# Attention and top-1 experts on one core: the leftover rows of an expert move into that expert's own pass, small units share one tile, and the fallback leaves GpSimd out

## The chip, the core and the metric

The kernel runs on one core of a Trainium2 chip. The metric is device time in microseconds; the kernel before has a median of 573.84 us over three runs. The profile is one further execution of the same kernel, with a span of 555.2 us between its first and last instruction, and all times inside the kernel are counted from the start of that span. The engines are TensorE (PE in the profile, its weight loads PEld), VectorE (DVE), ScalarE (ACT), GpSimd (POOL) and SyncE (SP). A `q` behind an engine's name stands for its sequencer, which handles waits, branches and register work.

## The reference

A banded attention is followed by a layer of eight experts, of which each token uses one. Cut to what matters:

```python
def reference(...):
    # attention: q, k, v of (4 batches, 8 heads, 768 positions, 64)
    scores = q @ k.T / 8 + bias           # per head a slope times the distance
    a = softmax(where(is_global | is_local, scores, -1e9))   # 8 global keys, 96 local ones
    x = (a @ v) -> (3072, 512)            # heads side by side
    # experts
    logits = x @ w_gate                   # (3072, 8)
    expert = argmax(logits)               # one expert per token
    gate = softmax(logits)[expert]
    for e in range(8):
        rows = x[expert == e]
        out[expert == e] = gate * (relu(rows @ w1[e]) @ w2[e])   # 512 -> 1024 -> 512
```

Everything is fp32.

## The kernel before

The kernel first does the attention and the routing (0 to about 168 us in the profile), writing each token's row to a table in DRAM, sorted by expert. A row of that table has 516 words: 512 of x, the gate, the token's number and two of padding. Two single tiles of 128 rows, of experts 0 and 1, are taken early. Then come eight passes, one per expert. A pass handles 256 rows (two tiles) with a recursive matrix product that trades multiplications for additions; that is `up_a`, `up_b` (first layer) and `down_a`, `down_b` (second layer). What an expert has beyond that is done by plain products, in units of 128, 64 and 32 rows. Which of the units are needed is a number from 0 to 7, the form: bit 4 for the unit of 128 rows, bit 2 for that of 64, bit 1 for that of 32. It depends on the data, so the kernel has a body of code for each form and chooses with a jump table, the switch.

```python
    def gather_u(self, e):                       # rows of the units, from DRAM
        for i in range(3):                       # 128, 64 and 32 rows: a tile each
            self.gather(self.xs[:, i, :], self.grow[:, e, 2 + i:3 + i])

    def x_units(self):                           # transposes on TensorE
        banks = self.t
        for c in range(NDC):                     # NDC = 4
            nc.tensor.transpose(banks[0][:, c, :], self.xs[:, 0, ts(c, P)], ident[:])      # L1136
        for s, cols in self.COLS.items():        # s = 1: 64 rows, s = 2: 32 rows
            n = P >> s
            for c in range(NDC):
                nc.tensor.transpose(banks[1][:, c, cols], self.xs[0:n, s, ts(c, P)],       # L1140
                                    ident[0:n, 0:n])
        nc.scalar.copy(self.xsT[0][:], banks[0][:])
        nc.scalar.copy(self.xsT[1][:, :, r], banks[1][:, :, r])                            # L1143

    def units(self, e, k, banks, between):       # the body for form k
        small = [s for s in (1, 2) if k >> 2 - s & 1]
        big = range(2 if k & 4 else 0)
        for s in small:
            ...  matmul into ph                                                            # L1157
            nc.scalar.activation(self.hr[s - 1][:], ph, AF.Relu)
        for half in big:
            ...  up_s (L853), relu
        between[0]()                             # a part of the pass's own work
        for s in small:
            ...  transpose hr (L1168), copy on ScalarE
        between[1]()                             # another part of it
        for half in big:
            self.down_s(e, self.huT, half, banks[2])                                       # L863
        ...
        for s in small:
            ...  matmul into py (L1182), scaled by the gate on ScalarE (L1185)

    def hint(self, e):                           # asks for a prefetch of the body to come
        if e < E:
            tc.switch_hint({PE: self.forms[e]}, FORMS, label=f"units{e}")

    def by_form(self, e, banks, between):
        for k in tc.Switch({eng: self.forms[e] for eng in self.ENGINES}, FORMS, hint=f"units{e}"):
            self.units(e, k, banks, between)     # ENGINES = (PE, ACT)
        self.hint(e + 1)
        self.send_u(e)                           # three scatters on GpSimd

    def passes(self, judge):
        for e in range(E):
            ...  up_a(e, 0), up_a(e, 1)
            if e == 0:
                self.x_units(); self.meta_u(0); self.gather_u(1)
            ...  up_b(e, 0), up_a(e, 2), up_b(e, 1)
            parts = lambda: (self.up_a(e, 3), self.up_copy(3)), lambda: self.up_b(e, 2)
            if e == 0:
                self.by_form(0, self.u[0:2] + self.d, parts)     # expert 0's units
            ...
            if more:
                self.x_units(); self.meta_u(e + 1)               # the NEXT expert's units
                if e + 2 < E: self.gather_u(e + 2)
            ...  up_b(e, 3), h_combine(1)
            parts = (first half of down_a, second half of down_a)            # L1076
            if more:
                self.by_form(e + 1, self.u, parts)               # the NEXT expert's units
            ...
            if more: self.x_in(e + 1); self.x_combine()          # L994
            self.gated(e); self.down_b(e)                                    # L1085
            ...  results, weights of e + 2 fetched
            for t in range(2): self.send(e, t)                   # scatters on GpSimd, L793
```

So pass 0 has two switches, passes 1 to 6 one each, for the next expert, and pass 7 none. After the passes, a flag is read on every engine, and where the fast path is not valid for the data, a general version runs:

```python
    flag = nc.values_load(bad_i[0:1, 0:1], min_val=0, max_val=1, ...)          # L1345, all engines
    with tc.If(flag > 0, preferred_fallthrough_block=False):                   # L1347
        again = Route("_g")
        ...  general(stack, again)       # attention anew, uses GpSimd
        ...  experts(stack, again, wpool)
```

With the reference's inputs the flag is zero and the general version is not run.

Of the kernel before, what the change touches and what calls it, by code (L numbers as in the profile page):

```python
# [23 lines left out]
def kernel(  # L24
# [28 lines left out]
    NA = E  # L53
    NB = NTOK // P - 1
    JT = NA + NB
# [82 lines left out]
    def weights(wpool, expert):  # L138
        w1t = wpool.tile([P, NDC, F], F32, tag="w1", name="w1t")
        w2t = wpool.tile([P, NFC, DM], F32, tag="w2", name="w2t")  # L140

        def fill():
            for dst, src, n in ((w1t, moe_w1, NDC), (w2t, moe_w2, NFC)):
                s = src[ds(expert, 1)].rearrange("o (c p) f -> p (o c) f", p=P)
                for a in range(0, n, n // 2):
                    nc.sync.dma_start(out=dst[:, a:a + n // 2, :], in_=s[:, a:a + n // 2, :])

        return w1t, w2t, fill


# [21 lines left out]
    def choose(pool, rt, xr, lg):  # L172
# [13 lines left out]
        def gates():  # L186
            nc.scalar.activation(sh[:], sh[:], AF.Exp)
            se = pool.tile([P, NBLK], F32, tag="se", name="se")
            nc.vector.tensor_reduce(se[:], sh[:], AX.X, ALU.add)
            nc.vector.tensor_scalar(se[:], se[:], 1e-9, None, ALU.add)  # L190
            nc.vector.reciprocal(xr[:, :, DM:DM + 1], se[:].unsqueeze(2))
            nc.vector.tensor_copy(out=xr[:, :, DM + 1:DM + 2].bitcast(I32), in_=rt.tokid[:].unsqueeze(2))
            nc.vector.tensor_scalar(rt.tokid[:], rt.tokid[:], S, None, ALU.add)

        return oh, gates
# [293 lines left out]
    def block_logits(pool, ps, wg, xr, lg, i):  # L489
        pt = ps.tile([P, NDC, P], F32, tag="t", name="pt")  # L490
        for c in range(NDC):
            nc.tensor.transpose(pt[:, c, :], xr[:, i, ts(c, P)], ident[:])
        xt = pool.tile([P, NDC, P], F32, tag="xt", bufs=2, name="xt")
        nc.scalar.copy(xt[:], pt[:])
        pl = ps.tile([P, 512], F32, tag="t", name="pl")
        for c in range(NDC):
            nc.tensor.matmul(pl[:, 0:E], lhsT=xt[:, c, :], rhs=wg[:, c, :],
                             start=(c == 0), stop=(c == NDC - 1))
        nc.vector.tensor_copy(out=lg[:, i, :], in_=pl[:, 0:E])


    def general(stack, rt):
        wg = stack.enter_context(tc.tile_pool(name="wg", bufs=1)).tile([P, NDC, E], F32, name="wg")
        nc.scalar.dma_start(out=wg[:], in_=moe_w_gate.rearrange("(c p) e -> p c e", p=P))
        pool, rows = router_pools(stack)
        seq = stack.enter_context(tc.tile_pool(name="seq_g", bufs=1))
        work = stack.enter_context(tc.tile_pool(name="work_g", bufs=2))
        ps_s = stack.enter_context(tc.tile_pool(name="ps_sg", bufs=2, space=bass.MemoryType.PSUM))
# [4 lines left out]
        key = seq.tile([P, S], F32, name="key_g")  # L513
        nc.gpsimd.iota(key[:], pattern=[[1, S]], base=0, channel_multiplier=0,
                       allow_small_or_imprecise_dtypes=True)

        with tc.For_i(0, B, 1) as b:
            kt = seq.tile([P, NPAIR, S], F32, name="kt_g")
            qt = seq.tile([P, NPAIR, S], F32, name="qt_g")
            vt = seq.tile([P, NBLK, H, D], F32, name="vt_g")  # L520
            for i in range(NBLK):
                for nm, src, dst, on, scale in (("k", k, kt, "dve", 1.0), ("q", q, qt, "act", QS)):
                    r = work.tile([P, H, D], F32, tag=nm, name=f"raw_{nm}g")
                    nc.sync.dma_start(out=r[:], in_=src[ds(b, 1), :, ts(i, P), :].rearrange(
                        "o h p d -> p (o h) d"))
                    transposed(ps_t, dst[:, :, ts(i, P)], r, on, scale)
                nc.sync.dma_start(out=vt[:, i], in_=v[ds(b, 1), :, ts(i, P), :].rearrange(
                    "o h p d -> p (o h) d"))
            xr, lg = new_rows(rows)
            units = [(i, h) for i in range(NBLK) for h in range(H)]  # L530
            st = {}

            def scores(u):
                i, h = units[u]
                if h == 0:
                    rel = work.tile([P, S], F32, tag="rel", name="rel_g")
                    nc.gpsimd.iota(rel[:], pattern=[[-1, S]], base=i * P, channel_multiplier=1,
                                   allow_small_or_imprecise_dtypes=True)
                    st["mask"] = mask(work, rel[:], key[:], S)
                    st["sums", i] = work.tile([P, H], F32, tag="sums", name="sums_g")  # L540
                keep, dist, neg = st["mask"]
                m, r = h // 2, slice(D * (h % 2), D * (h % 2) + D)
                sp = ps_s.tile([P, 2, 512], F32, tag="s", name="sp_g")
                for a in range(2):
# [46 lines left out]
    def experts(stack, rt, wpool):  # L591
# [120 lines left out]
        with tc.manual_schedule(engines={PE}):  # L712
# [5 lines left out]
            for j in range(JT):  # L718
# [3 lines left out]
                if j:  # L722
                    down(j - 1)
# [660 lines left out]
```

## Time and profile before

| | |
|---|---|
| median of 3 runs | 573.84 us (571.16 to 578.95) |
| span of the profiled execution | 555.2 us |
| attention and routing, 0 to about 190 us | TensorE busy 179.42 of 190.00 us |
| 190.0 to 254.5 us, early tiles and pass 0 | TensorE busy 56.59 of 64.50 us |
| 254.5 to 511.0 us, passes 1 to 6 | TensorE busy 251.19 of 256.50 us |
| 511.0 to 555.0 us, pass 7 and the end | TensorE busy 24.73 of 44.00 us |
| transposes of the small units (L1140) | 64 matmul records, 6.6 us |
| GpSimd's gathers of the units' rows (L785, `xs`) | 24, mean 1148 ns of GpSimd each |

How to read it: an engine's share of busy time is an average over stages. TensorE is nearly always busy in passes 1 to 6, less in pass 0 and not at all in the last 19 us. The profile counts neither branches nor waits nor register work as busy; they are found in the trace under the line they belong to. Those of the switch's dispatch and exit, and those of the closing of the program, all carry the kernel's last line, L1379.

### The profile page before, as it was taken

The numbers are of one execution on the slowest core, as the hardware profiler recorded it, in microseconds if no ns is written. First come the engines' busy times: TensorE is split into PE (matmuls) and PEld (weight loads), VectorE is DVE, ScalarE is ACT, GpSimd is POOL, SyncE is SP. The second block draws the span as 40 slices with busy tenths as digits, with TensorE's granted clock in tenths as the row PEclk, the third lists the DMA queues.
The fourth block names the chain that finished last, engine by engine and source line by source line (L and its number), as shares of the span: only waits on it lengthen the run. The fifth ranks groups of instructions, "written<-read, shape, count | busy, mean of one in ns | idle before, by whom it ended". The sixth has DMA issues, their size and how long they took to land.

```text
span 555.2 us, 12977 instructions
## 1 busy us (share of the span) xinstructions
PE 511.9 (92%) x5377; PEld 435.9 (79%) x5377; DVE 301.5 (54%) x638; ACT 146.2 (26%) x281; POOL 160.0 (29%) x242
## 2 busy tenths in 40 slices
PE   5899999999999999679999999999899999997950
PEld 4788898888987786469969969978787996987940
DVE  5566866767865451626708706817804641764810
ACT  3544555444441012111202211211211211221210
POOL 5200231311514560633206206306303411603010
PEclk9999999999999999899999999999999999998995
DMA  9998999999961320524524506506503621600010
GB/s 179 216 197 198 252 255 208 223 269 242 236 203 77 101 79 21 183 84 153 182 77 169 170 1 238 201 4 227 198 2 115 215 87 32 220 3 32 13 44 2
DMA packets 99314, 77.84 MB, mean 140 GB/s; under 512 B 80054, under 2 KB 80056, under 8 KB 99200
## 3 DMA queue, kind: packets, MB, share of 16 engines
q1 hardware_dynamic: 90368, 56.63, 40.0%
q0 software_dynamic: 8000, 19.77, 10.6%
q8 instruction: 59, 0.97, 0.8%
q14 instruction: 55, 0.45, 0.3%
q10 hardware_dynamic: 832, 0.02, 0.1%
HBM read 63.54 MB, written 14.73 MB: 141 GB/s over the span
## 4 chain that ended last, share of the span: by engine, by line
PE 86%; DVE 4%; issue 3%; ACT 2%; DMA 1%; POOL 0%; ACTq 0%; POOLq 0%; DVEq 0%
PE u L1014 18%; PE d L1076 10%; PE u L853 9%; PE sp L358 7%; PE d L1085 7%; PE po L387 6%; PE u L863 6%; PE pt L239 4%; PE pr L398 3%; PE u L1157 3%; PE u L1182 3%; PE d L863 3%; PE px L417 2%; PE t L994 1%; DVE p L372 1%
## 5 line engine op out<-in xcount | busy, mean ns | idle before, releaser
L372 DVE TENSOR_TENSOR p<-sp,other 128x1024 f32<-128x1024 f32 x40 | 47.1, 1219 | 33.7 <-PE sp L358 31.8
L1092 DVE TENSOR_TENSOR UV<-UV,d 128x512 f32<-128x512 f32 x8 | 5.5, 687 | 103.5 <-ACT yu L1185 70.4
L793 POOL DMA_INDIRECT out_dram<-ys,to_u x8 | 8.3, 1038 | 154.5 <-ACT yu L1185 115.8
L853 PEld LDWEIGHTS u<-xsT,w 128*128 128x128 f32 x448 | 50.7, 192 | 1.7 <-DVE ch L1062 0.8
L853 PE MATMUL u<-xsT,w 128*128 128x128 f32 x448 | 51.7, 276 | 0.0
L1014 PE MATMUL u<-cx,c 128*128 128x128 f32 x384 | 48.1, 275 | 0.0
L1014 PEld LDWEIGHTS u<-cx,c 128*128 128x128 f32 x384 | 45.5, 192 | 0.0
L379 ACT ACTIVATE p<-p 128x1024 f32<-128x1024 f32 (+1 forms) x48 | 44.5, 977 | 2.1 <-DVE p L372 2.0
L358 PE MATMUL sp<-qt,kt 64*128 64x128 f32 x448 | 39.0, 281 | 1.4 <-DVE kt L244 1.4
L1014 PE MATMUL u<-xT,w 128*128 128x128 f32 x256 | 40.1, 279 | 0.1
L785 POOL DMA_INDIRECT xs<-xs_dram,grow x24 | 27.5, 1148 | 34.8 <-PE t L1140 28.9
L387 PE MATMUL po<-p,vt 128*64 128x128 f32 x448 | 37.1, 274 | 0.0
L1014 PEld LDWEIGHTS u<-xT,w 128*128 128x128 f32 x256 | 34.2, 192 | 1.9 <-issue 0.7
L300 POOL COPY ka<-kt 128x384 f32<-128x384 f32 x16 | 8.2, 511 | 93.7 <-DVE den_all L423 90.7
L863 PE MATMUL u<-w,huT 128*128 128x512 f32 x80 | 35.1, 592 | 0.0
L358 PEld LDWEIGHTS sp<-qt,kt 64*128 64x128 f32 x448 | 31.9, 193 | 3.4 <-ACT qt L242 1.6
L1076 PE MATMUL d<-c,ch 128*128 128x256 f32 x128 | 32.8, 379 | 0.0
L1045 DVE TENSOR_TENSOR uv<-uv,u 128x256 f32<-128x256 f32 x32 | 13.4, 420 | 31.4 <-ACT uv L1041 18.3
L219 POOL DMA_INDIRECT xs_dram<-xr,slot_i x24 | 23.7, 986 | 22.6 <-DVE base_e L217 9.8
L1041 ACT COPY uv<-u 128x256 f32<-128x256 f32 x32 | 11.9, 372 | 68.4 <-PE u L1014 68.3
L863 PEld LDWEIGHTS u<-w,huT 128*128 128x128 f32 x80 | 15.2, 190 | 17.0 <-issue 16.7
L793 POOL DMA_INDIRECT out_dram<-y,to x16 | 18.1, 1134 | 35.3 <-DVE y L1103 31.3
(233 smaller groups left out, 1057.4 us busy)
## 6 DMA issues: line engine op xcount, KB each, us to landing
w<-in_moe_w_dram SPq DMA_DIRECT2D x24, 1024.0 KB, 5.6
w<-in_moe_w_dram SPq DMA_DIRECT2D x16, 512.0 KB, 6.3
raw_q<-in_q_dram SPq DMA_DIRECT2D x24, 256.0 KB, 5.4
raw_k<-in_k_dram SPq DMA_DIRECT2D x24, 256.0 KB, 5.4
vt<-in_v_dram SPq DMA_DIRECT2D x24, 256.0 KB, 6.2
va<-vt SPq DMA_DIRECT2D x16, 192.0 KB, 5.6
va<-vt SPq DMA_DIRECT2D x16, 64.0 KB, 5.2
xs_dram<-xr,slot_i POOLq DMA_INDIRECT x24, 6.2
```

What stands on the lines that cost most here:

```text
L219: d = nc.gpsimd.indirect_dma_start(out=xs_dram[:], out_offset=bass.IndirectOffsetOnAxis(ap=slot_i[:, u:u + 1], axis=0), in_=xr[:, u, :].bi ...
L358: nc.tensor.matmul(sp[:, a, j, t, :], lhsT=kt[r, m, :], rhs=qts[n][r, m, :], start=True, stop=True, skip_group_check=True)
L372: nc.vector.tensor_tensor(z, sc, bi, ALU.add)
L379: nc.scalar.activation(z, z, AF.Exp)
L387: nc.tensor.matmul(po[D * a:D * a + D, m, :], lhsT=vt[:, 2 * m + a, :], rhs=ps[n][m // 2][:, a, m % 2, t, :], start=(x == 0), stop=(x == l ...
L785: nc.gpsimd.indirect_dma_start(out=dst.bitcast(I32), out_offset=None, in_=xs_dram[:], in_offset=bass.IndirectOffsetOnAxis(ap=idx, axis=0), ...
L793: d = nc.gpsimd.indirect_dma_start(out=out.rearrange("n (g d) -> (n g) d", g=parts), out_offset=bass.IndirectOffsetOnAxis(ap=idx, axis=0), ...
L853: nc.tensor.matmul(ph[:, i, :], lhsT=self.w[e % 2][0][:, c, ts(half * HF + i, P)], rhs=xT[:, c, :], start=(c == 0), stop=(c == NDC - 1), s ...
L863: nc.tensor.matmul(py[:].rearrange("p a b -> p (a b)"), lhsT=h[:, f, :], rhs=self.w[e % 2][1][:, f, :], start=(f == 0), stop=(f == NFC - 1 ...
L1014: nc.tensor.matmul(bank[:, r, :], lhsT=lhs(k), rhs=rhs(k), start=first, stop=True, skip_group_check=True)
L1076: nc.tensor.matmul(self.half(i, j), lhsT=lhs, rhs=rhs, start=(f == 0 and j == 0), stop=True, skip_group_check=True)
L1085: nc.tensor.matmul(self.half(i, j), lhsT=lhs(f), rhs=rhs(f), start=False, stop=True, skip_group_check=True)
```

## The change

The change has four parts.

* **Own expert's form.** Pass e now runs the units of expert e, not of e + 1, in its second-layer stage. Every pass has exactly one switch, in the same place, and pass 0's extra switch is gone.
* **Small units in one tile.** The rows of the 64-row and the 32-row unit are gathered into one tile of 96 rows, so that 4 transposes do for both. The gates and token numbers are wanted on partitions 0 to 63 and 0 to 31, so they are gathered a second time, into a small tile `mu`, 4 words a row.
* **Forms rotated.** Body number k of the switch now holds form (k + 6) mod 8, so the bodies lie in memory in the order 6, 7, 0, 1, 2, 3, 4, 5.
* **Fallback without GpSimd.** The general version is written anew, unrolled, without any GpSimd work, and the flag is read on the other four engines only.

The core of the diff:

```diff
         def gather(self, dst, idx):
+            n = dst.shape[-1]
             nc.gpsimd.indirect_dma_start(
-                out=dst.bitcast(I32), out_offset=None, in_=xs_dram[:],
+                out=dst.bitcast(I32), out_offset=None, in_=xs_dram[:].rearrange("r (a b) -> (r a) b", b=n),
...
+            nc.vector.tensor_copy(out=k_i[:], in_=k[:])
+            nc.vector.tensor_scalar(k[:], k[:], float(FORMS - FIRST), None, ADD)     # FIRST = 6
             nc.vector.tensor_copy(out=self.form[:], in_=k[:])
+            nc.vector.tensor_scalar(self.form[:], self.form[:], FORMS - 1, None, ALU.bitwise_and)
...          (seven small VectorE operations that make the indices grow_m and grow_e)
         def gather_u(self, e):
-            for i in range(3):
-                self.gather(self.xs[:, i, :], self.grow[:, e, 2 + i:3 + i])
+            self.gather(self.xs[:, 0, :], self.grow[:, e, 2:3])
+            self.gather(self.xs[:, 1, :], self.grow_m[:, e:e + 1])
+            for i in (1, 2):
+                self.gather(self.mu[:, i, :], self.grow_e[:, e, i - 1:i])

         def meta_u(self, e):
-            f = self.to_f
-            nc.gpsimd.tensor_copy(out=f[:], in_=self.xs[:, :, DM + 1].bitcast(I32))
+            f, mu = self.to_f, self.mu
+            nc.gpsimd.tensor_copy(out=mu[:, 0, :], in_=self.xs[:, 0, DM:XW])
+            nc.gpsimd.tensor_copy(out=f[:], in_=mu[:, :, 1].bitcast(I32))
...
-            for s, cols in self.COLS.items():
-                n = P >> s
-                for c in range(NDC):
-                    nc.tensor.transpose(banks[1][:, c, cols], self.xs[0:n, s, ts(c, P)], ident[0:n, 0:n])
+            n = self.COLS[2].stop
+            for c in range(NDC):
+                nc.tensor.transpose(banks[1][:, c, 0:n], self.xs[0:n, 1, ts(c, P)], ident[0:n, 0:n])
...
-        def by_form(self, e, banks, between):
+        def by_form(self, e, between):
             for k in tc.Switch({eng: self.forms[e] for eng in self.ENGINES}, FORMS, hint=f"units{e}"):
-                self.units(e, k, banks, between)
+                self.units(e, (k + FIRST) % FORMS, between)
...
-                if e == 0:
-                    self.x_units()
-                    self.meta_u(0)
-                    self.gather_u(1)
...
-                parts = lambda: (self.up_a(e, 3), self.up_copy(3)), lambda: self.up_b(e, 2)
-                if e == 0:
-                    self.by_form(0, self.u[0:2] + self.d, parts)
-                else:
-                    for part in parts:
-                        part()
+                self.up_a(e, 3)
+                self.up_copy(3)
                 self.up_add(3)
                 self.up_22(1)
+                self.up_b(e, 2)
                 c2[2]()
                 self.up_end(2)
+                self.x_units()
+                self.meta_u(e)
                 if more:
-                    self.x_units()
-                    self.meta_u(e + 1)
-                    if e + 2 < E:
-                        self.gather_u(e + 2)
+                    self.gather_u(e + 1)
...
-                if more:
-                    self.by_form(e + 1, self.u, parts)
-                else:
-                    for part in parts:
-                        part()
+                self.by_form(e, parts)
...
-    flag = nc.values_load(bad_i[0:1, 0:1], min_val=0, max_val=1,
+    engines = (PE, ACT, DVE, SP)
+    flag = nc.values_load(bad_i[0:1, 0:1], engines=engines, min_val=0, max_val=1,
                           skip_runtime_bounds_check_because="a count, cut off at one")
-    with tc.If(flag > 0, preferred_fallthrough_block=False):
-        again = Route("_g")
-        with ExitStack() as stack, tc.manual_schedule(engines={PE}):
-            general(stack, again)
+    with tc.If(flag > 0, preferred_fallthrough_block=False), tc.manual_schedule(engines=set(engines)):
         with ExitStack() as stack:
-            wpool = stack.enter_context(tc.tile_pool(name="wpool_g", bufs=2))
-            experts(stack, again, wpool)
+            general(stack)
```

The general version itself, not run here, is left out of the diff above.

## The prediction

> **What bounds the kernel now.** I began with the busy times and the summary of the chain that ended last.
>
> ```profile
> PE 511.9 (92%) x5377; PEld 435.9 (79%) x5377; DVE 301.5 (54%) x638; ACT 146.2 (26%) x281; POOL 160.0 (29%) x242
> PE 86%; DVE 4%; issue 3%; ACT 2%; DMA 1%; POOL 0%; ACTq 0%; POOLq 0%; DVEq 0%
> ```
>
> TensorE is busy 511.9 of 555.2 us. So there are three ways to gain: fewer TensorE instructions, fewer of its gaps, or a shorter end. The second view is TensorE's waits from 198 us on, where the expert passes begin; the last two columns are the count and the longest wait.
>
> ```profile
> PE t L994 <- issue: 7.1, 5, 3.5
> PE u L1157 <- ACT xsT L1143: 4.1, 1, 4.1
> PE u L1157 <- ACT h L1060: 1.6, 1, 1.6
> PE t L1136 <- issue: 0.3, 1, 0.3
> ```
>
> These 13.1 us are nearly all the waiting in the passes, and each lies at the entry or exit of a switch: L1157 is the first product in a body, L994 the first after one. So I read the branches, which are filed under the kernel's last line, L1379 (columns: ns min/median/max, first and last start).
>
> ```profile
> L1379 PEldq COMPARE_BRANCH  x16: 293/309/4649, 206.3 to 499.3; - x16
> L1379 POOLq DRAIN  x3: 46/107/8973, 545.4 to 554.9; - x3
> ```
>
> Sixteen branches are eight entries and eight exits. Most take 0.3 us; taken singly, four are long: 4.65 us at 224.7 (entry for expert 1, in pass 0), 3.56 at 242.3 (its exit), 2.98 at 394.8 (entry for expert 5), 3.61 at 499.3 (exit for expert 7). The chain around the first two:
>
> ```profile
> 224.81 1.55 PE u L1014 x12
> ...
> 229.84 0.49 ACT xsT L1143
> 230.34 0.14 issue
> 230.47 3.45 PE u L1157 x32
> ...
> 243.76 2.84 issue
> 246.60 1.34 PE t L994 x8
> ```
>
> The L1157 group of 32 takes 3.45 us here and 1.86 in pass 6 (at 489.05). The reason is in windows set just behind the three longest gaps; the third column from the end is the granted TensorE clock, 0.50 in each:
>
> ```profile
> 230.18:233.60 3.42, 3.13 (x32) 1.57 (x32) 3.28 (x5) 0.46 (x2) 2.81 (x3) 0.50 0.49 148
> 247.25:250.66 3.41, 3.41 (x11) 2.82 (x10) 3.27 (x7) 0.91 (x2) 2.83 (x5) 0.50 0.48 117
> 503.25:506.66 3.41, 3.41 (x13) 3.03 (x13) 2.37 (x4) 0.53 (x2) 1.79 (x4) 0.50 0.07 16
> ```
>
> A gap of 3 us or more thus costs itself plus about 3.4 x 0.5 = 1.7 us. The 1.63 us gap at 396.5 is followed by no such window.
>
> The third place is the end. The last product ends near 535.7, the last scatter's work on GpSimd at 536.99 + 0.98 = 537.97, yet the span ends at 555.2. What lies between is in the conditional's line and in the 8.97 us drain above, which starts at 545.35:
>
> ```profile
> L1347 POOLq EVENT_SEMAPHORE  x5: 17/42/2842, 537.0 to 540.2; - x5
> L1347 POOLq COMPARE_BRANCH  x2: 33/39/45, 536.9 to 542.6; - x2
> L1347 POOLq INC_SWDGE_SEM  x1: 2339/2339/2339, 540.2 to 540.2; - x1
> ```
>
> GpSimd waits for its DMAs (2.84), adjusts their semaphores (2.34), jumps over the fallback (542.6 to 545.35), drains (8.97), and only then does the closing barrier run (0.83).
>
> **What the skill says.** The Trainium skill, "TensorE: Matmul & The Clock Gate", Part 1, says the array drops to half its clock after an idle window of about 3.4 us and needs a busy one to recover. The trace agrees: gaps of 4.13, 3.47 and 2.97 us each give 3.4 us at 0.50. "Runtime: NRT & Kernel Launch", Instruction fetch mechanics, says that the stream comes in 16 KiB blocks of 256 instructions and that a taken branch whose target isn't there forces a fetch. The trace agrees: the instruction queue that serves TensorE moved 59 packets and 0.97 MB, 16 KB each, and a long branch is about 3 us longer than a short one. "DMA: Bandwidth & Descriptors", Anatomy of one DMA, gives GpSimd-issued DMAs about 2 us of fixed cost; here the scatters took a median 3.7 us to land, beside 1.0 us of GpSimd.
>
> **The change part by part.** The forms must be known. Routing the reference's inputs gives 455, 416, 361, 397, 367, 410, 395 and 271 rows. After the first single tile of experts 0 and 1 (128 rows each) and the two-tile pass (256), the forms are 3, 1, 4, 5, 4, 5, 5, 1 (bit 4: a 128-row unit; 2: 64 rows; 1: 32 rows).
>
> *One switch per pass.* Pass 0 now holds two switches, expert 0's and expert 1's; pass 7 holds none. After, each pass has its own. The products are the same eight sets, so TensorE's work does not change, but one defect goes. Expert 1's entry comes 1.4 us after its prefetch hint (223.24 to 224.67), because the two switches nearly touch. After, the hint stands a whole upward stage ahead, as in passes 1 to 6. Gain 4.13 + (3.45 - 1.86) = 5.7 us.
>
> *What stays.* Form 1's two exits stall (3.56 and 3.61), forms 3, 4 and 5 do not. I count form 1's body as 66 products of fp32, each two weight loads and two matmuls: 264 instructions, just over one block of 256. A prefetch of the exit that begins when the last block is entered gets only a dozen instructions of lead. Form 4 has 56 products (224, one block), form 5 has 106 (424, 168 into its second). The rotation moves bodies about and changes no body's length, so both stalls remain, now in passes 1 and 7: 0.
>
> *Entry of expert 5* (1.63 us): by the same reasoning an accident of where the branch falls in a block. The four transposes fewer, and the moved switch, shift every entry. With about 45 of 256 positions bad, eight entries give 1.4 stalls, some 2.3 us each with a share of half clock: 3.2 against 1.6 now. Loss 1.5 us.
>
> *Small rows in one tile.* Per expert, 4 transposes of 64 rows and 4 of 32 become 4 of 96. The eight take 0.75 us in the chain (at 224.06), four of 128 rows take 0.63. With their lead-in I take 0.32 us off each: 8 x 0.32 = 2.5 us gain.
>
> *Gathers.* Three become four, two of them of 16 bytes a row, plus one copy: 8 x (1.12 + 0.2) = 11 us more of GpSimd. It is busy 29%, and these gathers have nearly a pass to land in: 0 on the path. The table gets about ten small VectorE operations; VectorE stood idle 8.3 us before the copy of the first x tile: 0.
>
> *Weights.* Expert e's first-layer weights are now read until pass e's switch, so the load for e+2 begins later (about 335 instead of 305 us, in pass 2's place). Expert e+2's earliest use moves too, to the combinations at the end of pass e+1. 4 MB at the observed 250 to 400 GB/s is 10 to 16 us of some 40: 0.
>
> *Fallback without GpSimd.* It is not run. But GpSimd no longer loads the flag, waits for its DMAs, adjusts semaphores or jumps. Its drain can start at about 538.1 instead of 545.35: 7.2 us earlier, if it keeps its 8.97 us. I take 7.
>
> Sum: 5.7 + 2.5 - 1.5 + 7 = 13.7 us. From the median of 573.84 that is 560.1; I say 560. The profiled execution would have a span of about 541.5 instead of 555.2.
>
> **The rivals.** *The drain is not a fixed cost.* If it waits for the last scatters to land (3.3 us) and then takes its 9, the end gains 4, not 7: 563. If the semaphore adjustment caused its length, only SyncE's wait for the landings remains, and the end gains 11 or more: 556. That it still took 9 us after all data had landed speaks for a fixed cost; the length of the other two drains, 0.1 us and less, speaks against one.
>
> *New stalls at the switches.* Two more entries that miss at about 4.7 us each with the half clock would eat most of the gain: 568. For it: four of sixteen branches miss now. Against: the two at form 1 and the one of pass 0 have their own causes, so that only one in seven is accidental.
>
> *ScalarE becomes late.* Its entries fetch too, taking 2.2 to 6.3 us, and its relu feeds form 1's transposes after only 1.9 + 3.6 us of TensorE work. In pass 6 it made it with 2 us to spare. A slow fetch in passes 1 and 7 would add up to 3 us each. The long fetches lie where weights are in flight (397 to 402, for instance), and the later load takes weights away from the entries, so I put little on this; it may even help.
>
> **Range and chances.** The two sure pieces (5.7 and 2.5) make 8.2 us; the end adds 4 to 12; stalls take 0 to 6. That is 6 to 20 us, 554 to 568. The times before spread over 571.16 to 578.95, which widens it to 551 to 568. Faster by over 2% needs 11.5 us, some 2 below my sum: 0.67. Within 2%: 0.30. Slower needs a stall in nearly every pass: 0.03.
>
> **What would show it.** Pass 0 without a gap near 226 us and one half-clock window fewer; eight branches at entry, none of 4 us; the transposes of the small rows half in number; TensorE's busy time down by about 4 us (2.5, and 1.6 of the half clock); the GpSimd drain starting within 1 us of the last scatter's work; no semaphore adjustment there. Two exit stalls of about 3.6 us left, in passes 1 and 7. I am wrong if the drain grows by what was taken from in front of it, or if other entries begin to stall.

## The result, and the profile after

The changed kernel takes a median of 554.58 us (550.89 to 556.94, four runs) against 572.80 us (571.16 to 578.95, four runs) for the kernel before. The ratio is 0.966, with a 95% interval of 0.956 to 0.975, so 14 to 25 us are gained. The predicted 560.0 lies 5.4 us above the measured time, the range of 551 to 568 holds it; the predicted gain of 13.7 us is just too small for the interval.

The first view of the page after, the busy times:

```profile
PE 512.0 (93%) x5345; PEld 435.2 (79%) x5345; DVE 303.5 (55%) x650; ACT 146.2 (27%) x281; POOL 172.3 (31%) x259
```

TensorE has 32 matmul records less, as it must with 8 x 4 transposes fewer, and GpSimd has 12.3 us more, as predicted (11). Yet TensorE's busy time is the same, and the span of this profile is 549.1 us, only 6.1 below the 555.2 of the profile that I predicted from. The reason is the attention, which the change does not touch. Its waits, 60 to 198 us, after:

```profile
PE pr L385 <- issue: 7.4, 14, 1.0
```

In the profile before no such line stands among the waits of that stage. The first upward product of the passes begins at 198.62 us there and at 214.78 here. A second profile of the kernel before, below, settles this: it belongs to the chip that a run lands on, not to the kernel. The stages of the two kernels are therefore compared in a pair of profiles of one chip. In that pair TensorE's busy time does fall, from 523.2 to 515.1 us, by 8 us where 4 were predicted.

TensorE's waits in the passes, and behind them the branches of the switch on its queue with GpSimd's drains, after (columns as before the change: us in all, count, longest; ns min/median/max, first and last start):

```profile
PE t L900 <- DMA out_dram<-ys,to_u: 6.3, 1, 6.3
PE d L991 <- issue: 2.7, 1, 2.7
```

```profile
L1271 PEldq COMPARE_BRANCH  x16: 294/309/6295, 226.5 to 532.0; - x16
L1271 POOLq DRAIN  x3: 45/108/4868, 541.6 to 547.3; - x3
```

The wait for expert 1's first product (4.1 us) and the one at expert 5's entry (1.6) are gone. What is left are form 1's two exits, in passes 1 and 7 as predicted, but the first has grown from 3.5 to 6.3 us. The waits' view gives it to a scatter; that is only the transfer that happened to end last before it. The branch itself takes 6.295 us, and that is the cause. The half clock behind it, in a window set at its end (third column from the end), is there too:

```profile
284.15:287.55 3.40, 3.40 (x12) 3.09 (x13) 2.08 (x3) 0.11 (x1) 1.20 (x2) 0.50 0.76 270
```

At the end of the program the drain is 4.87 us instead of 8.97, and starts at 541.6, before the last scatter's work is over. Nothing of GpSimd's wait, adjustment and jump is left.

### The profile page after: what moved, and what is told of

Read it like the earlier page. It is cut to its first block, busy times and chain, and to the rows that moved or that the text cites. A ratio compares the mean times of both kernels' runs of the same rounds, so it can differ in the third digit from the quotient of the medians.

```text
span 549.1 us, 12930 instructions
## 1 busy us (share of the span) xinstructions
PE 512.0 (93%) x5345; PEld 435.2 (79%) x5345; DVE 303.5 (55%) x650; ACT 146.2 (27%) x281; POOL 172.3 (31%) x259
## 3 DMA queue, kind: packets, MB, share of 16 engines
q0 software_dynamic: 7872, 19.01, 10.0%
## 4 chain that ended last, share of the span: by engine, by line
PE 70%; issue 15%; POOL 4%; DVE 3%; ACT 2%; DMA 2%; another core or an unknown queue 1%; POOLq 0%; SPq 0%; ACTq 0%
PE u L920 13%; PE u L746 9%; PE sp L345 8%; PE d L982 6%; PE u L756 6%; PE d L991 6%; PE po L374 6%; PE pr L385 4%; PE pt L226 4%; DVE p L359 2%; POOL out_dram L680 2%; PE px L404 1%; PE t L900 1%; PE pr L390 1%; PE d L756 1%
## 5 line engine op out<-in xcount | busy, mean ns | idle before, releaser
L385 PE MATMUL pr<-p,one_in 128*32 128x128 f32 x704 | 29.9, 285 | 8.2 <-issue 7.4
L385 PEld LDWEIGHTS pr<-p,one_in 128*32 128x32 f32 x704 | 19.9, 112 | 15.8 <-issue 13.9
L947 ACT COPY uv<-u 128x256 f32<-128x256 f32 x32 | 11.9, 373 | 65.0 <-PE u L920 49.9
L229 ACT ACTIVATE qt<-pt 128x512 f32<-128x512 f32 x24 | 14.4, 598 | 52.3 <-PE pt L226 49.0
```

The source lines that it names most:

```text
L385: nc.tensor.matmul(pr[GW * m:GW * m + GW, 0, :], lhsT=one_in[:, a, :], rhs=ps[n][m // 2][:, a, m % 2, t, :], start=(x == 0), stop=False, s ...
```

## The experiments

Three stages are read from each trace: the start of the first upward product of the passes; from there to the end of the last downward product; and from there to the end of the span. "Transfers" are those that GpSimd issues and that run.

| kernel | start of passes | passes | end | transfers |
|---|---|---|---|---|
| before, first profile | 198.6 | 337.1 | 19.5 | 108 |
| after, first profile | 214.8 | 326.2 | 8.1 | 116 |
| before_again | 218.2 | 336.2 | 19.3 | 108 |
| after_again | 219.3 | 323.8 | 8.0 | 116 |
| pool_dma | 217.5 | 326.2 | 7.5 | 116 |
| short_body | 218.0 | 322.0 | 6.7 | 116 |
| before_new_fb | 199.0 | 337.0 | 12.0 | 108 |
| many_dma | 199.6 | 329.6 | 8.0 | 116 |
| tail_work | 199.8 | 318.0 | 6.8 | 116 |
| no_fetch3 | 202.2 | 323.8 | 6.6 | 116 |
| three_tiles | 219.4 | 337.1 | 11.5 | 108 |
| before_plus8 | 216.9 | 339.4 | 9.8 | 116 |
| before_plus4 | 199.6 | 335.2 | 20.1 | 112 |
| no_rotation | 200.1 | 327.5 | 7.8 | 116 |

### Both kernels once more, on one chip

No edit. Expected of the kernel before:

> The kernel before, profiled once more, unchanged. The changed kernel's profile spends 214.8 us up to its first upward product of the passes, that of the kernel before 198.6, though both have the same attention; three places of about 5 us each account for it, each just behind six scatters of routed rows. Theory A (such places are the rule in both kernels, and the first profile of the kernel before missed them): here the passes start at about 210 to 216 us, and the span is 568 to 574. Theory B (the change brought them): the passes start at 198.6 +- 2 us again, and the span is about 555.

and of the changed one:

> The changed kernel, profiled once more. Theories A and B: the passes start at about 210 to 216 us. Theory C (chance per execution): they may start near 199, with a span of about 533. In all of them the passes take 326 us from the first upward product to the end of the last downward one, and the end behind that 8 us.

Measured: 575.53 and 552.87 us. The waits of the attention, 60 to 198 us, kernel before:

```profile
PE pr L398 <- issue: 7.5, 13, 1.0
```

The same 7.5 us stand there now, and the passes start at 218.2 us. Theory A holds, in a sharper form: the six kernels that ran on this chip start their passes at 216.9 to 219.4 us, the six on two other chips at 199.0 to 202.2, whichever code they hold. My first profile of the kernel before came from the second kind.

So on one chip, 573.7 - 551.1 = 22.6 us of span divide into 12.4 in the passes (336.2 - 323.8), 11.3 at the end (19.3 - 8.0) and -1.1 before. The prediction had 6.7 for the passes (5.7 + 2.5 - 1.5) and 7 for the end. The longest waits of TensorE in the passes, kernel before and then after:

```profile
PE t L994 <- issue: 6.7, 5, 3.3
PE u L1157 <- ACT xsT L1143: 3.6, 1, 3.6
```

```profile
PE t L900 <- issue: 5.1, 5, 4.2
PE d L991 <- issue: 3.0, 1, 3.0
```

The pair is one execution of each kernel. Expert 1's exit branch happens to be 4.28 us long in it; in the first profile after, where it took 6.29, the passes took 326.2 us, as they do in pool_dma. With such an exit 20.2 of the 22.6 us would be left, nearer to the 18.2 between the medians.

### The end: the fallback alone

The kernel before with the new fallback and nothing else of the change (before_new_fb):

```diff
-    flag = nc.values_load(bad_i[0:1, 0:1], min_val=0, max_val=1, ...)
-    with tc.If(flag > 0, preferred_fallthrough_block=False):
-        ...  general(stack, again); experts(stack, again, wpool)
+    engines = (PE, ACT, DVE, SP)
+    flag = nc.values_load(bad_i[0:1, 0:1], engines=engines, min_val=0, max_val=1, ...)
+    with tc.If(flag > 0, ...), tc.manual_schedule(engines=set(engines)):
+        ...  general(stack)
```

> The kernel before with one part of the change alone: the new fallback without GpSimd, the flag read on four engines. Theory (the end's gain is its own and does not depend on the other parts): from the last downward product to the end of the span 8 us instead of 19.4, the passes 336 to 337 us as before; about 0.980 of before (11.4 of 576 us). Rival (part of the end's gain came with the new order of the passes, for instance since the last scatters stand alone): 12 to 15 us at the end, 0.988 or more.

Measured: 549.45 against 557.11 us, a ratio of 0.988 (0.983 to 0.993). The end shrinks from 19.4 to 12.0 us, that is by 7.4. The drain in this kernel:

```profile
L1271 POOLq DRAIN  x3: 45/108/10547, 536.6 to 547.7; - x3
```

It starts at 536.59 and ends at 547.14. The last scatter's work ends at 537.25 + 0.98 = 538.23, so 8.9 us are still spent behind it, as many as the drain took before. The rival is right: the fallback alone is worth 7.4 us, which is the prediction's "7.2 us earlier, if it keeps its 8.97 us", and something else in the change makes the drain itself shorter.

### The end: GpSimd back in the conditional

The changed kernel, with GpSimd reading the flag again and one load of the fallback moved to it (pool_dma):

```diff
-    engines = (PE, ACT, DVE, SP)
+    engines = (PE, ACT, DVE, POOL, SP)
...
-        nc.scalar.dma_start(out=wg[:], in_=moe_w_gate.rearrange("(c p) e -> p c e", p=P))
+        nc.gpsimd.dma_start(out=wg[:], in_=moe_w_gate.rearrange("(c p) e -> p c e", p=P))
```

> The changed kernel, in which GpSimd again reads the flag and takes part in the conditional, and the (not run) fallback issues one of its loads from GpSimd. From the end of the last downward product to the end of the span the changed kernel takes 8.1 us, that before 19.5. Theory (GpSimd's part in a conditional that holds DMAs of its own causes wait, semaphore adjustment, jump and the long drain together): the end takes 17 to 20 us again, the drain 8 to 9, and the time is 9 to 12 us above the changed kernel's, about 565 (0.985 to 0.99 of before). Rival (only wait, adjustment and jump return, about 7 us, and the drain stays at 5): the end takes 13 to 15 us, about 560. Third (the old fallback's other GpSimd work was the cause): the end stays at 8 to 9 us, 554.

The same with 68 such loads instead of one (many_dma):

```diff
+        for i in range(17):
+            for c in range(NDC):
+                nc.gpsimd.dma_start(out=wg[:, c, :], in_=moe_w_gate[ts(c, P), :])
```

> The changed kernel, whose GpSimd takes part in the conditional again, and whose fallback (not run) issues 68 loads from GpSimd, as many transfers as the old fallback's code held. With a single one, the end was not longer than the changed kernel's (7.5 against 8.1 us, the semaphore adjustment 0.37, the drain 3.27). Theory (adjustment and drain grow with the number of skipped transfers): the adjustment takes 2 us or more, the drain 8 to 9, the end 17 to 20 us. Rival (the old fallback's loop, its indirect transfers or its other GpSimd work caused both): the end stays at 7.5 to 9 us.

Measured: 554.73 us for the first (0.964 of before, 0.960 to 0.969), 539.28 for the second (before: 557.11 on that chip). Semaphore adjustment and drain of the second:

```profile
L1245 POOLq INC_SWDGE_SEM  x1: 388/388/388, 534.4 to 534.4; - x1
```

```profile
L1273 POOLq DRAIN  x3: 51/107/893, 534.9 to 536.4; - x3
```

The end stays at 7.5 and 8.0 us. GpSimd's part in the conditional costs the changed kernel nothing, and what the skipped code holds plays no part. My theory falls: the 8.97 us of drain are no price of a conditional. The adjustment does come back with it, but takes 0.37 and 0.39 us here, so its 2.34 us were no fixed price either.

### The end: the number of GpSimd's transfers

What had changed besides was the number of transfers: 108 before, 116 with the second, small gathers. The first edit takes those out of the changed kernel (three_tiles), the second puts eight small gathers, whose rows nothing reads, into the kernel before (before_plus8):

```diff
-            self.gather(self.xs[:, 0, :], self.grow[:, e, 2:3])
-            self.gather(self.xs[:, 1, :], self.grow_m[:, e:e + 1])
-            for i in (1, 2):
-                self.gather(self.mu[:, i, :], self.grow_e[:, e, i - 1:i])
+            for i in range(3):
+                self.gather(self.xs[:, i, :], self.grow[:, e, 2 + i:3 + i])
...  and the three sets of transposes as before
```

> The changed kernel with the small units' rows in separate tiles again, as before: 3 gathers per expert instead of 4 and 12 transposes instead of 8; 108 GpSimd transfers in all instead of 116. For the passes: the prediction's 0.32 us per expert, so 2.5 us more than the changed kernel's passes less their exit stalls (319.6 to 320 us in three profiles, so about 322.3); rival: no difference that is seen, 320. For the end: the new fallback alone, in the kernel before, left a drain that ends 8.9 us behind the last scatter's work; in the changed kernel it ends 3.7 us behind it, with the landing. Theory T (the long drain belongs to a program with 108 transfers, not to one with 116, that is to something the drain settles per transfer): the drain here ends 8.9 us behind the last scatter's work, the end takes 12 us. Rival U (it belongs to the order of the passes, with expert 7's units scattered 25 us or 3 us before the last scatters): the drain ends about 3.7 us behind, the end takes 7 to 8 us.

```diff
             for i in range(3):
                 self.gather(self.xs[:, i, :], self.grow[:, e, 2 + i:3 + i])
+            nc.gpsimd.indirect_dma_start(out=self.spare[:, e, :].bitcast(I32), out_offset=None,
+                in_=xs_dram[:].rearrange("r (a b) -> (r a) b", b=4),
+                in_offset=bass.IndirectOffsetOnAxis(ap=self.grow[:, e, 2:3], axis=0), ...)
```

> The kernel before with one more small gather per expert (16 bytes a row, into a tile that nothing reads): 116 GpSimd transfers instead of 108, everything else as before. Theory T (the drain's length depends on the number of transfers): the drain shrinks from 8.97 to about 1 us, as in the changed kernel with GpSimd in the conditional (0.89), and the end from 19.4 to about 11.5 us. Rival U (the order of the passes): the drain stays at 8.97, the end at 19.4.

With the second edit for experts 0 to 3 only (before_plus4):

> The kernel before with four more small gathers, of experts 0 to 3 only: 112 GpSimd transfers. With 108 the adjustment took 2.34 us and the drain 8.97, with 116 they took 0.39 and 0.98. Theory (each transfer short of some mark costs about 1 us at the end): adjustment and drain together 5 to 8 us, the end 13 to 16 us. Rival (a threshold between 108 and 116): together either 11.3 or 1.4 us, the end 19.4 or 9.8 us.

Drain of the changed kernel with 108 transfers:

```profile
L1270 POOLq DRAIN  x3: 45/108/10117, 557.1 to 567.7; - x3
```

Adjustment and drain of the kernel before with 116 transfers, and then with 112:

```profile
L1354 POOLq INC_SWDGE_SEM  x1: 388/388/388, 561.0 to 561.0; - x1
```

```profile
L1386 POOLq DRAIN  x3: 46/107/978, 564.2 to 565.8; - x3
```

```profile
L1354 POOLq INC_SWDGE_SEM  x1: 2428/2428/2428, 539.6 to 539.6; - x1
```

```profile
L1386 POOLq DRAIN  x3: 46/107/9307, 544.7 to 554.6; - x3
```

Theory T holds both ways. The changed kernel with 108 transfers has the long drain back: it ends at 557.05 + 10.12 = 567.17, 8.9 us behind the last scatter's work (557.29 + 0.97), and the end takes 11.5 us. The kernel before with 116 transfers loses it: 0.98 us instead of 8.97, adjustment 0.39 instead of 2.34, end 9.8 instead of 19.3, and the time is 567.82 against 576.57 us, with eight gathers more and nothing taken away. The order of the passes has no part in it. With 112 transfers nothing is gained, so it is a step and not a slope. From 108 to 112 both lengths grow in proportion: 8.97/108 and 9.31/112 are both 0.083 us a transfer, 2.34/108 and 2.43/112 both 0.0217. What counts is the transfers and not the packets in GpSimd's DMA queue: the long drain came with 8000 and 8128 packets, the short one with 7872 and 8256. Each of these runs is a single one, but the drain took 8.973 us in both profiles of the kernel before, so differences of 8 us are no chance.

So the end's 11.3 us are, taken in this order, 7.4 by the fallback and 3.9 by the eight gathers (three_tiles against the changed kernel gives 3.5). The two cure the same ill: with the gathers alone 9.5 us are gained, and with 116 transfers GpSimd may as well stay in the conditional.

### The small units' rows

The run three_tiles also shows what the shared tile is worth in the passes. The chain through one expert (5), after, from one set of x transposes (L900) to the next; columns: start, us, what:

```profile
412.51 0.87 PE t L900 x8
...
430.38 0.33 PE t L1048 x4
430.72 1.37 PE u L920 x12
...
457.38 1.06 PE t L900 x8
```

and the same stretch with separate tiles:

```profile
419.86 0.88 PE t L900 x8
...
437.75 0.75 PE t L1046 x8
438.50 1.53 PE u L920 x12
...
465.33 1.06 PE t L900 x8
```

44.87 against 45.47 us: 0.60 us per expert, 4.8 in all. Three other stretches of this kind, between earlier sets, differ by 0.58 to 0.59. Of it 0.42 lies in the transposes (0.75 to 0.33) and 0.16 in the products behind them. The whole passes of this run, 337.1 us, are no measure of it: they hold a gap of 2.7 us in pass 5's last products and an entry of 0.87 us at expert 6, both new, the first of them with a half clock behind it.

### The exits of form 1

The prediction read the two exit stalls as those of a body that is just over one block of 256 instructions. Moving 8 products (32 instructions) ahead of the switch makes it 232 (short_body):

```diff
-                parts = (lambda: self.down_a(e, range(0, HF // 2)),
-                         lambda: (self.down_a(e, range(HF // 2, HF)), self.down_copy()))
+                self.down_a(e, range(0, HF // 2))
+                parts = (lambda: self.down_a(e, range(HF // 2, HF - 1)),
+                         lambda: (self.down_a(e, range(HF - 1, HF)), self.down_copy()))
                 self.by_form(e, parts)
```

> The changed kernel, in which the first half of the first downward stage (8 products, 32 instructions of TensorE) stands ahead of the switch instead of in its body, so that the body of form 1 has 232 instead of 264 instructions, one block of 256 instead of two. TensorE's work is the same. Theory (the exit of form 1 stalls since its prefetch is asked for only on entry into the body's last block, a dozen instructions from its end): the gaps of 6.3 and 2.8 us behind the switches of passes 1 and 7 vanish with their half-clock window, 9 to 13 us together; about 543 (0.945 to 0.95 of before). Rival (the exit stalls come from weight traffic or from the position of the exit in memory, not from the body's length): both gaps stay, 552 to 557.

Measured: 549.02 us, 0.952 of before (0.946 to 0.959). Its waits in the passes, and its branches:

```profile
PE t L900 <- issue: 3.6, 5, 2.8
PE u L920 <- DVE uv L951: 2.1, 1, 2.1
PE d L991 <- ACT yu L1092: 0.6, 1, 0.6
```

```profile
L1272 PEldq COMPARE_BRANCH  x16: 288/298/2891, 231.4 to 533.1; - x16
```

Taken singly, the exits for experts 1 and 7 now take 0.30 and 0.32 us, where they took 4.3 to 6.3 and 3.4 to 3.7. The theory holds for form 1. But half of the gain went elsewhere. Form 3's body (328 instructions) now stalls at its exit for 2.89 us: what lies behind its first block are short products, and counted from their records, 1.0 us passes from there to the exit, against 2.3 in the changed kernel. The packets of TensorE's instruction queue, 16 KB each, agree: the one ahead of this exit starts 0.58 us behind the branch, where in the first profile after it started 2.19 us ahead of it. Two entries take 1.4 us that took 0.3. And VectorE's checks for the fallback now hold up the products of pass 2 for 2.1 us. VectorE takes as long as in the changed kernel, 11.8 to 11.9 us, from TensorE's first transposes behind expert 1's exit to the end of this work; but TensorE's products in between had taken 12.0 us with the half clock and take 9.8 without, so that they no longer cover it.

The next edit moves only 4 products ahead, so that form 1 has 248 instructions, and puts the last 4 at the end of the body, where they stretch form 3's second block (tail_work):

```diff
+                self.down_a(e, range(0, 1))
+                parts = (lambda: self.down_a(e, range(1, 2)), lambda: self.down_a(e, range(2, 3)),
+                         lambda: (self.down_a(e, range(3, HF)), self.down_copy()))
...
                 nc.scalar.activation(self.yu[s - 1][:], py, AF.Copy, bias=0.0, scale=gate[:, s:s + 1])
+            between[2]()
```

> The changed kernel with the first of four chunks of the first downward stage (4 products, 16 instructions) ahead of the switch and the last of them behind the units' products, at the end of the body. With 8 products ahead, form 1's exits no longer stalled, but form 3's did (2.8 us), since only 1.0 us of short products was left between its entry into the body's second block and its exit; VectorE's checks then held up pass 2 for 2.1 us. Theory (an exit is ready if the body fits one block, or if at least 2.5 us of work lie behind the block's end): form 1 (248 instructions) and form 3 (344, of which 16 slow ones last) both leave within 0.5 us; the passes take 314 to 319 us instead of 324 to 326; 542 to 548 (0.943 to 0.952 of before). Rival (each edit only moves the stall to another switch): some exit or entry stalls 2.5 us or more again, the passes stay at 322 or more.

Measured: 524.38 against 557.11 us, 0.942 of before (0.938 to 0.946): the fastest of all. Waits in the passes, and branches:

```profile
PE u L920 <- DVE uv L951: 1.9, 1, 1.9
PE t L900 <- issue: 0.5, 1, 0.5
```

```profile
L1273 PEldq COMPARE_BRANCH  x16: 288/307/2297, 212.6 to 510.0; - x16
```

Form 1 leaves in 0.30 and 0.31 us. Form 3's branch still takes 2.30, so 2.5 us of work behind the block's end was not enough of a lead, against my theory (its packet starts 0.25 us ahead of the branch); but TensorE waits only 0.5 us for it, since the long products are still in its queue. One entry, expert 3's, takes 1.77 us.

The packets show the same for every switch. In the fourteen traces 48 of its branches take over 0.5 us, and 47 of these end 1.3 to 1.6 us behind the end of the last packet (the other, in before_plus8, 2.3). In bodies of up to 248 instructions two packets follow the entry, the second within 4 to 8 us; in longer ones the second comes 12 us or more behind the entry, and at form 1's exits with 264 instructions only 0.6 us or more behind the branch. That fits the prediction's reading, by which the exit is asked for on entry into the last block, but the lead of a dozen instructions that it gave form 1 is not seen: the fetch begins when the branch already waits.

### Weights, and the order of the bodies

Why has expert 1's exit grown? The load of expert 3's weights into the same buffers starts at 277.6 us after the change, half a microsecond after the branch that leaves the switch (277.1). Without that load (no_fetch3; expert 3's pass then works with expert 1's weights, so the run leaves out the load and its result):

```diff
-                        self.fetch(e + 2)
+                        if e != 1:
+                            self.fetch(e + 2)
```

> The changed kernel without the load of expert 3's weights at the end of pass 1 (4 MB; expert 3's pass then works with expert 1's weights, so this run leaves work out). In the changed kernel the exit of expert 1's switch takes 6.3, 4.3 and 6.4 us in three profiles, in the kernel before 3.6 and 3.4; expert 7's exit, where no weights are loaded, takes 3.1 to 3.7. Theory (the instruction fetch stands behind the weights, whose load now starts just as the switch ends): expert 1's exit takes 3.1 to 3.7 us. Rival (its length comes from where the code lies): 4.3 to 6.4 us as before.

```profile
L1272 PEldq COMPARE_BRANCH  x16: 293/305/3757, 213.9 to 516.9; - x16
```

Measured: 534.61 us. The longest branch is now 3.76 us, at expert 1's exit; with the load it took 6.29, 4.28, 6.37, 6.12, 6.42 and 4.16 us in six profiles of kernels that have this switch unchanged. The theory's upper limit of 3.7 is just missed, and this is a single run. But the instruction packets say the same. With the load, the packet for this exit starts 3.7 to 4.0 us behind the branch in four of the six profiles, and in the other two it starts after 0.6 us and takes 2.1 and 2.3. Without the load it starts after 1.40 us and takes 0.94; at expert 7's exit, where no weights are loaded, it starts after 0.6 to 1.0 us and takes 0.9 to 1.3.

The last of the four parts of the change is the rotation. With the forms in their old order (`FIRST = 0`, no_rotation):

> The changed kernel with the forms in their old order, so that the switch's bodies lie in memory as 0, 1, 2 ... 7. Theory of the prediction (moving bodies about changes no body's length and so no stall): the exits of form 1 (experts 1 and 7) take 4 to 6.5 us and 3.1 to 3.7 us, the others 0.3 to 0.5, no entry more than 0.5; the passes take 323 to 327 us. Rival (the rotation puts an often used body beside the code that follows and saves fetches): one or more other entries or exits stall by 1.5 us or more, the passes take 328 or more.

```profile
L1271 PEldq COMPARE_BRANCH  x16: 293/306/4159, 211.8 to 515.5; - x16
```

Measured: 537.20 against 554.91 us on that chip. The exits of form 1 take 4.16 and 3.60 us, all entries 0.29 to 0.35. The passes take 327.5 us, half a microsecond over the range named, 3 us of it in a half clock that lasted longer behind expert 7's exit. No stall came or went: the rotation does nothing that is seen here.

## Why the prediction was right where it was, and wrong where it was

By its own steps, in the pair of profiles on one chip:

| step | predicted, us | measured, us |
|---|---|---|
| one switch per pass: expert 1's entry | 5.7 | 5.0 (gap 3.62, products 3.21 - 1.86) |
| small rows in one tile | 2.5 | 4.8 |
| entries as a lottery (expert 5's and others) | -1.5 | +1.5 |
| exits of form 1 and the later weights | 0 | -1.2 (3.29 to 4.18, 2.75 to 3.02) |
| fallback without GpSimd | 7 | 7.4 |
| gathers | 0 | +3.9 |
| not assigned | | 2.3 in the passes, -1.1 before them |
| sum | 13.7 | 22.6 |

*What held.* "Expert 1's entry comes 1.4 us after its prefetch hint": with the hint a whole stage ahead the branch takes 0.3 to 0.4 us in every profile after, and its half clock is gone. But the hint was not the whole of it: TensorE's branch was over at 224.67 + 4.65 = 229.32, and the products waited on until 230.47 for ScalarE's copy (229.84 to 230.32), as the prediction's own line of that wait says. ScalarE had issued nothing for 5.8 us behind its own branch out of expert 0's switch. The change parts the two switches for both engines, so no run shows what TensorE's hint alone is worth. Form 1's exits stayed, in passes 1 and 7, for the reason given: the body's length decides, as short_body and tail_work showed. The Trainium skill, "Runtime: NRT & Kernel Launch", Instruction fetch mechanics, states the blocks of 256; that 264 instructions stall and 248 do not is this case's own number. The fallback's 7.2 us came out at 7.4, with the drain at its old length, just as assumed.

*Where sizes were off.* "I take 0.32 us off each" rested on 0.63 us for four transposes, read from the set that comes first. Behind another set, four of 96 rows take 0.33, and the products behind them gain 0.16 more: the term measured 0.60. The lottery ("eight entries give 1.4 stalls") was drawn for a kernel whose entries are fixed: all eight were ready in every profile after. As an expectation it was not foolish, for each of three other edits brought one or two slow entries (0.87 to 1.77 us); but a mean of 1.4 may well be 0.

*Where a step was wrong.* "Weights ... 0": I asked only whether they arrive in time, and not what else wants the DMA engines when they start. They start at the moment of expert 1's exit, and the block of instructions that TensorE needs comes later for it: the gap is 0.9 us longer in this pair, 2.8 in the first profiles.

"Gathers ... 0 on the path": they are off the path and still moved the end by 3.9 us, for they took the number of transfers over the mark at which the drain becomes short. The rival that I wrote down, "if the semaphore adjustment caused its length, only SyncE's wait for the landings remains, and the end gains 11 or more", named the right size for a wrong cause. Nothing in the profile before pointed to the number of transfers; it said only that the drain, 8.97 us after all data had landed, was no wait for data.

In the pair, 8.9 us more were gained than the sum had. Missing in it are the transfers (3.9), the entries (3.0), the small rows (2.3), the unassigned part of the passes (2.3, of which 0.7 is a wait of pass 0's transposes for ScalarE that came with the extra switch) and 0.4 at the fallback; against it stand the exits (1.2), expert 1's entry (0.7) and the stage before the passes (1.1). By the medians it is 18.2 against 13.7 us: the direction and the main terms were right, most of them too small. The 3.9 us of the transfers come from a cause that the prediction did not have. That the rest of the gain, some 14 us, lies so near its 13.7 is in part luck, since errors of both signs meet in it.

## What to carry to other kernels

Look at what stands behind the last useful instruction, and test it by itself: here 19 of 573 us were a drain and its lead-up, and eight idle gathers removed half of it. Count the instructions of a switch's body: here bodies of 232 and 248 let TensorE leave at once and one of 264 did not, and with four slow products at the end of a longer body TensorE waited 0.5 us for a branch of 2.3. When one stall is removed, work that it had covered (VectorE's checks here) comes to light. Before two profiles are subtracted, compare a stage that the change does not touch; if that differs, take both on one chip.

## What the runs showed of the hardware that was not expected

* The closing drain of GpSimd, and the semaphore adjustment ahead of a conditional, last 0.083 and 0.0217 us per transfer that GpSimd has issued, at 108 and at 112, and are 0.9 to 1.0 and 0.37 to 0.39 us in all at 116, where the data had landed before. (Where the drain began ahead of the landings, it holds that wait too: 3.3 to 5.1 us at 116.) The Trainium skill, "DMA: Bandwidth & Descriptors", SWDGE vs HWDGE vs iDMA, says that GpSimd writes the descriptors of its transfers into rings in SBUF; a ring that starts anew between 112 and 116 would fit, but this is only argued, and no run here shows it. Where the step lies exactly, and whether it comes again, stays open.
* A branch of the switch that had to wait ended 1.3 to 1.6 us behind the end of its 16 KB instruction packet in 47 of 48 cases, and a 4 MB load of weights that started 0.55 us behind such a branch put its end off by up to 2.7 us (3.76 us without the load, 4.16 to 6.42 with it).
* One chip of three ran the same attention 15 to 20 us slower than the other two. Most of it lies in three places, each beginning 4 to 6 us into the six scatters of a batch's rows, where TensorE issues 32 small products (L385, before L398) in dribbles: in 4.2 to 6.0 us, where the others take about 1.0. What holds it there was not tried.
* A gap of nearly 3 us is not always followed by the same half clock: behind expert 7's exit, the window of 3.4 us at the end of a 2.75 us gap shows 1.00 in the profile after, and behind 2.83 us in many_dma 0.50, then 0.59 in the window that follows; behind 2.70 us in three_tiles it is 0.51. So the prediction's "3 us or more" is no sharp limit here. From expert 7's exit branch to the end of the last product it is 9.0 us in the one and 12.1 in the other.

```profile
535.60:539.00 3.40, 3.40 (x16) 3.01 (x17) 0.48 (x1) 0.91 (x2) 1.85 (x2) 1.00 0.05 10
```

```profile
520.70:524.10 3.40, 3.35 (x8) 2.73 (x9) 0.48 (x1) 0.85 (x2) 1.81 (x2) 0.50 0.06 10
524.10:527.50 3.40, 3.40 (x10) 2.69 (x10) 0.00 (x0) 0.00 (x0) 0.00 (x0) 0.59 0.04 12
```

The first fence is of the kernel after, the second of many_dma; the third column from the end is the granted clock.
